# Attention pairs of four groups spread over both products of the groups before them, in a fused attention and feed-forward kernel

## The chip, the cores and the metric

The kernel runs on one core of a Trainium2 chip. The time is that of one execution on the device, in microseconds (us). Three runs of the kernel before gave 254.63, 254.75 and 253.64 us, a median of 254.63. A fourth execution was taken with the hardware profiler: 253.48 us, with 251.8 us from the first to the last instruction (the span). Of the engines, PE is TensorE (its weight loads are PEld), DVE is VectorE, ACT is ScalarE, POOL is GpSimd and SP is SyncE, which here only issues transfers.

## What is computed

Sliding-window attention with four sink keys, and behind it a two-layer network on all tokens:

```python
# q, k, v: (4 batches, 8 heads, 768 positions, 64), n_sink 4, window 128
scores = scale * np.matmul(q, k.transpose(0, 1, 3, 2))
keep = is_sink | in_window            # 0 <= row - column < 128, or column < 4
scores = np.where(keep, scores, -1e9)
a = np.exp(scores - np.max(scores, axis=-1, keepdims=True))
a = a / (np.sum(a, axis=-1, keepdims=True) + 1e-09)
attn = np.matmul(a, v)
x = attn.transpose(0, 2, 1, 3).reshape(3072, 512)
h = x @ w_in                          # 512 -> 2048
g = h * (1.0 / (1.0 + np.exp(-1.702 * h)))
out = g @ w_out                       # 2048 -> 512
```

## The kernel before

The 3072 tokens are cut into 12 groups g of 256 (two blocks i of 128); three groups t make one batch b. The eight heads are taken as four pairs hp. Everything stands in an order written out by hand: each engine runs its instructions in the order in which the program names them, so an instruction that waits holds all that stands behind it on that engine.

What one group needs, with the helper that issues it:

- `load_qk`, `load_v`: GpSimd issues the loads of 128 KB parts (line 124). `transposed_qk` (line 150 on) turns q and k: for g < EARLY = 3 by transposes on PE (L161) and copies by ACT (L163) and DVE (L165), for later groups by a DMA transpose on SP's queue (L154).
- `sinks(g)`: scores against the four sink keys on PE (L192), their scaled negatives and minima on DVE (L201 or L197, L203).
- `scores(g, hp)`: eight matmuls of a pair (L233, masks by L231) into PSUM. Groups in SPLIT (1 and 2) put the block before the diagonal into two `pr` tiles of the tag "av" and the block on the diagonal into a "nat" tile that two pairs share; other groups use one whole "nat" tile for a pair. There are two buffers of each tag: "nat", "av", and "mm" for the two products.
- `maxima(g, hp)` on DVE: the window chosen by a predicated copy (L247, or twice L256), the row maximum (L250, or L259) and the bias (L260).
- `weights(g, hp)` on ACT: four exponentials of 128x128 (L271). `sink_terms` (DVE, L302) and `sink_weights` (ACT, L311) do the same for the sink keys of all four pairs at once; `sink_transposed` turns them on PE (L316), with a copy on DVE (L318).
- `weights_transposed(g, hp, copy)`: on PE (L288) with a copy by DVE (L294) or ACT (L297), or without `copy` by a DMA transpose on SP's queue (L291).
- `upper` on POOL (L347) and `lower` on DVE (L329) or POOL cut the transposed weights into the two triangles. `values` (PE, L360, L368, L372) multiplies them with v; `normal` (DVE, L389, L390) divides.
- `x_transposed(g)` turns the attention output: on PE with one copy by ACT and one by DVE (L402, L404, L406) for g < EARLY, else by DMA (L408).

Then come the two products of a group. `hidden(g, F2)` for F2 = 0 to 7 is sixteen matmuls (L420) and one gelu on ACT (L423); `o(g, i, parts)` is four matmuls for each of four parts of the contraction (L435). `out_store` copies the result by ACT (L441) or DVE (L443) and stores it.

The first and second product alternate on PE, and the attention of the next group is put between them. In this text, round n runs from the first matmul of `hidden(n, 0)` to that of `hidden(n+1, 0)`; its first stage is the first product and its second stage the second product, each with what stands between. Rounds 0 and 1 are written out one by one; from round 2's first stage on the loop `for n in range(EARLY, NG + LAG2)` writes them (its pass n holds the second product of group n-2 and the first of group n-1). In rounds 0 and 1 the scores and maxima of the next group stand in the first stage, and its weights, values and division in the second; round 1's second stage also makes the scores and weights of group 3. In the loop the attention of group n is one round deeper: its weights are made beside the second product of group n-2, and its values beside the first product of group n-1; the scores of pairs 0 and 1 of the group after stand in the first stage, those of pairs 2 and 3 in the second.

ACT needs one table for exponentials and another for gelu, so it loads a table twice in a round. `sink_columns(b)` clears a tile of 128x1040 and sets its ones columns (L478, L479): for batch 0 at the start, for batch 1 in round 0's second stage, for batches 2 and 3 ahead of the loop.

Of the kernel before, what the change touches and what calls it, by code (L numbers as in the profile page):

```python
# [10 lines left out]
FP32 = mybir.dt.float32  # L11
FP16 = mybir.dt.float16
# [7 lines left out]
TG = 256  # L20
BIG = 1.0e9
LAG1, LAG2 = 1, 2
SPLIT = (1, 2)
EARLY = 3


# [32 lines left out]
def kernel(  # L59
# [48 lines left out]
        return psp.tile(list(shape), dt, tag="av", bufs=2, name=name)  # L108

    G = [dict() for _ in range(NG)]  # L110

    def load_part(g: int, part: int):

# [33 lines left out]
    def transposed_qk(g: int, parts=range(2)):  # L147
# [17 lines left out]
                        nc.vector.tensor_copy(out=T[:, bass.ts(a, HP)], in_=tp)  # L165
        G[g]["qkT"] = T.rearrange("p (e i c) s -> p e i c s", e=2, i=2)

    def sink_keys(b: int, copy):
        kT = G[b * NT]["qkT"]
        for h in range(2):  # L170
            copy(
                out=kd[b][bass.ts(h, D), :, bass.ts(h, n_sink)],
                in_=kT[bass.ts(h, D), 1, 0, :, 0:n_sink],
            )
# [31 lines left out]
    def scores(g: int, hp: int):  # L206

        b, t = divmod(g, NT)  # L210
        qkT = G[g]["qkT"]
        if g in SPLIT:
            if hp < 2:
                G[g]["both", hp] = psp.tile([P, 2, 2, 2, P], FP32, tag="nat", bufs=2, name=f"nat{g}_{hp}")
            two = G[g]["both", hp % 2]
            before = [av_bank(f"pr{g}_{hp}_{h}", (P, 2, P)) for h in range(2)]
            mine = [two[:, h, hp // 2] for h in range(2)]
            G[g]["mine", hp] = two[:, :, hp // 2]
        else:
            whole = psp.tile([P, 2, 2, 2 * P], FP32, tag="nat", bufs=2, name=f"nat{g}_{hp}")  # L220
            before = [whole[:, h, :, 0:P] for h in range(2)]
            mine = [whole[:, h, :, P:] for h in range(2)]
            G[g]["whole", hp] = whole
        for i in range(2):
            I = 2 * t + i
            prev = None if I == 0 else qkT[:, 1, 0, hp] if i else G[g - 1]["qkT"][:, 1, 1, hp]
            for to, keys in ((before, prev), (mine, qkT[:, 1, i, hp])):
                for h in range(2):
                    r = bass.ts(h, D)
                    if keys is None:  # L230
                        nc.tensor.matmul(to[h][:, i], masked_l[r], masked_r[r], start=True, stop=True)  # L231
                    else:
                        nc.tensor.matmul(to[h][:, i], qkT[r, 0, i, hp], keys[r], start=True, stop=True)  # L233
        G[g]["nat", hp], G[g]["before", hp] = mine, before
# [61 lines left out]
    def by_act(out_, in_):  # L296
        nc.scalar.copy(out_, in_)  # L297

    def sink_terms(g: int):
        sn, bias = G[g]["sn"], G[g]["bias"]  # L300
        ts_ = work.tile([P, 16, n_sink], FP32, tag="ts", name=f"ts{g}")
        nc.vector.tensor_tensor(  # L302
            out=ts_, in0=bias.rearrange("p i c h -> p (i c h)").unsqueeze(2).broadcast_to((P, 16, n_sink)),
            in1=sn, op=ALU.subtract,
        )
        G[g]["ts"] = ts_

    def sink_weights(g: int):
        ts_ = G[g]["ts"]
        As = sinkA[g % 2]  # L310
        nc.scalar.activation(out=As[:, 0:64], in_=ts_.rearrange("p a j -> p (a j)"), func=AF.Exp)  # L311
        G[g]["As"] = As

    def sink_transposed(g: int):
# [79 lines left out]
    def x_transposed(g: int):  # L394
        xT = work.tile([P, 2 * HP, P], FP16, tag="xT", bufs=3, name=f"xT{g}")
        xn = G[g]["xn"].rearrange("p i a h d -> p (i a h d)")
        if g < EARLY:
            bank = mm_bank if g == 0 else av_bank
            for i in range(2):
                tp = bank(f"tx{g}_{i}", (P, HP, P), FP16)  # L400
# [57 lines left out]
    masked_l = const.tile([P, P], FP16, name="maskedl")  # L458
    masked_r = const.tile([P, P], FP16, name="maskedr")
    sinkA = [const.tile([P, P], FP16, name=f"sinkA{i}") for i in range(2)]  # L460
    nc.vector.memset(vs[0], 0.0)
    nc.vector.tensor_copy(out=vs[0][:, :, D : D + 1], in_=sink_rows.unsqueeze(2))
    nc.vector.memset(masked_l, -1000.0)
    nc.vector.memset(masked_r, 15624.0)
    for t_ in (*kd, *sinkA):
# [1 line left out]
    for row in vn:  # L467
        for t_ in row:
            nc.vector.memset(t_[:, :, :, D : D + 1], 1.0)
    zero_reg = nc.gpsimd.to_reg(0.0)  # L470
    load_w_in(0)
    load_qk(1)
    load_v(0)
    for i in (1, 2, 3):
        load_w_in(i)

    def sink_columns(b: int):
        nc.vector.memset(vs[b], 0.0)  # L478
        nc.vector.tensor_copy(out=vs[b][:, :, D : D + 1], in_=sink_rows.unsqueeze(2))  # L479

    def ahead(n: int, hp: int):

# [50 lines left out]
    load_w_out(0)  # L533
    load_w_out(1)
    load_v(1)
    load_w_out(2)
    load_w_out(3)
    load_qk(2)
    load_v(2)


# [6 lines left out]
    sink_terms(1)  # L548


    sink_weights(1)
    sink_columns(1)
    weights(1, 0)
    weights(1, 1)
    o(0, 0, 0)
    sink_transposed(1)
    o(0, 1, 0)
    weights_transposed(1, 0, by_dve)
    upper(1, 0)
    weights(1, 2)  # L560
    o(0, 0, 1)
    weights_transposed(1, 1, by_dve)
    upper(1, 1)
    load_part(3, 0)
    lower(1, 0)
    weights(1, 3)
    o(0, 1, 1)
    weights_transposed(1, 2, by_dve)
    upper(1, 2)
    load_part(3, 1)  # L570
    values(1, 0)
    lower(1, 1)
    normal(1, 0)
    o(0, 0, 2)
    weights_transposed(1, 3, by_act)
    upper(1, 3)
    lower(1, 2)
    values(1, 1)
    normal(1, 1)
    o(0, 1, 2)  # L580
    lower(1, 3)
    values(1, 2)
    normal(1, 2)
    o(0, 0, 3)
    values(1, 3)
    normal(1, 3)
    out_store(0, 0)
    o(0, 1, 3)
    x_transposed(1)
    out_store(0, 1, act=True)  # L590
# [1 line left out]
    load_part(3, 3)  # L592
    load_v(3)
    transposed_qk(3)
    sink_keys(1, nc.gpsimd.tensor_copy)
    load_qk(4)


    for F2 in range(NF // 2):
        hidden(1, F2)  # L600
        if F2 == 0:
            transposed_qk(2)
        if F2 in (1, 2, 4, 6):
            ahead(2, (1, 2, 4, 6).index(F2))
    sink_terms(2)


    sink_weights(2)
    for hp in (0, 2, 1, 3):
        weights(2, hp)  # L610
        weights_transposed(2, hp)
        upper(2, hp)
        if hp in (0, 2):
            lower(2, hp, pool=True)
    sink_values(1)
    o(1, 0, 0)
    sink_transposed(2)
    o(1, 0, 1, 2)
    ahead(3, 0)
    o(1, 0, 3)  # L620
    out_store(1, 0)
    o(1, 1, 0)
    weights(3, 0)
    weights_transposed(3, 0)
    transposed_qk(4)
    scores(3, 1)
    lower(2, 1)
    maxima(3, 1)
    o(1, 1, 1)
    for hp in (0, 2):  # L630
        values(2, hp)
        normal(2, hp)
    o(1, 1, 2)
    scores(3, 2)
    lower(2, 3)
    weights(3, 1)
    weights_transposed(3, 1)
    for hp in (1, 3):
        values(2, hp)
        normal(2, hp)  # L640
    o(1, 1, 3)
    out_store(1, 1, act=True)
    x_transposed(2)
    maxima(3, 2)
    scores(3, 3)
    maxima(3, 3)
    sink_terms(3)
    weights(3, 2)
    weights_transposed(3, 2)
    weights(3, 3)  # L650
    weights_transposed(3, 3)
    sink_weights(3)
    load_qk(5)
    lower(3, 0)
    transposed_qk(5)
    sink_columns(2)
    sink_columns(3)

    for n in range(EARLY, NG + LAG2):
        att = n < NG  # L660
        g1, g2 = n - LAG1, n - LAG2

        if n > EARLY:
            if att and n + 1 < NG and (n + 1) % NT == 0:
                sink_keys((n + 1) // NT, nc.gpsimd.tensor_copy)
            if n in (4, 5):
                load_v(n)
            if att:
                for hp in (0, 1):
# [90 lines left out]
```

## Time and profile before

| | |
|---|---|
| median of three runs | 254.63 us (253.64 to 254.75) |
| profiled execution | 253.48 us, span 251.8 us |
| PE busy | 220.5 us (88%), 2180 matmuls |
| DVE, ACT, POOL busy | 151.5 us, 153.9 us, 101.6 us |
| granted TensorE clock, mean | 0.991 |

The rounds begin, by the first matmul of L420 in each, at 24.53 (round 0), 46.44, 73.25, 95.10, 113.85 and 130.98 us (round 5). Their second stages begin at about 34.33, 57.82, 87.32, 105.09 and 123.20 us. Rounds 5 to 10 take 16.8 to 17.3 us each, round 0 21.9, round 1 26.8, round 2 21.9 and round 3 18.8 us.

The profiler lists busy times; the waits are inferred from semaphore events. A matmul's end is modelled and lies behind the start of the next one, so the cost of a run of matmuls is read from start to start.

### The profile page before, as it was taken

How to read it: one execution, taken by the hardware profiler on the slowest of the kernel's cores; microseconds unless marked ns; L12 is line 12 of the kernel's file. 1: busy time of each engine (PE TensorE's matmuls, PEld its weight loads, DVE VectorE, ACT ScalarE, POOL GpSimd, SP SyncE). 2: the span in 40 equal slices, each digit the busy share in tenths (PEclk: the TensorE clock that was granted, in tenths of full speed). 3: DMA queues.
4: the chain of work that ended last, by engine and by line, in shares of the span. 5: the costliest groups of instructions: out<-in, count | busy, mean ns of one | idle time of the engine just before them, and what ended most of it. 6: DMA issues, size and time to landing. Idle time of an engine off the chain costs nothing.

```text
span 251.8 us, 5731 instructions
## 1 busy us (share of the span) xinstructions
PE 220.5 (88%) x2180; PEld 151.2 (60%) x2180; DVE 151.5 (60%) x397; ACT 153.9 (61%) x349; POOL 101.6 (40%) x154
## 2 busy tenths in 40 slices
PE   0437979797785999999999999999999999799993
PEld 0326756674354848738758569478486595494851
DVE  4686777386589647657768288477583783830101
ACT  2176575748457577676766875776777767751430
POOL 8848547423662825816624445356020220310000
PEclk9999999999998899999999999999999999999999
DMA  8999999989699999999999989999965623603102
GB/s 77 157 176 198 188 194 123 160 107 98 116 144 175 153 131 169 165 119 246 115 158 160 144 169 144 133 172 140 163 131 98 108 63 64 146 3 83 42 3 85
DMA packets 133612, 32.86 MB, mean 131 GB/s; under 512 B 126288, under 2 KB 130512, under 8 KB 133584
## 3 DMA queue, kind: packets, MB, share of 16 engines
q0 software_dynamic: 79104, 13.64, 73.7%
q1 hardware_dynamic: 54048, 18.73, 42.2%
q8 instruction: 17, 0.28, 0.5%
q10 hardware_dynamic: 432, 0.13, 0.2%
q14 instruction: 11, 0.09, 0.1%
HBM read 27.50 MB, written 6.29 MB: 134 GB/s over the span
## 4 chain that ended last, share of the span: by engine, by line
PE 51%; DVE 17%; ACT 16%; DMA 10%; issue 4%; POOL 0%; ACTq 0%; DVEq 0%; POOLq 0%; SPq 0%
PE hT L420 27%; PE o L435 12%; ACT A L271 7%; DVE m L250 5%; DVE nat L247 5%; DMA AT<-A 5%; ACT L423 4%; DMA xT<-xn 3%; PE av L372 2%; ACT L271 2%; ACT gT L423 2%; DMA qkn<-in_q_dram 2%; PE av L360 2%; PE av L368 2%; PE tqk L161 1%
## 5 line engine op out<-in xcount | busy, mean ns | idle before, releaser
L420 PE MATMUL hT<-xT,w_in 128*128 128x256 f16 x768 | 95.6, 275 | 5.4 <-ACT gT L423 2.4
L435 PE MATMUL o<-w_out,gT 128*128 128x512 f16 x384 | 89.6, 379 | 0.0
L420 PEld LDWEIGHTS <-w_in 128*128 128x128 f16 x768 | 72.8, 99 | 18.6 <-issue 3.5
L423 ACT ACTIVATE gT<-hT 128x512 f16<-128x512 f32 x96 | 56.5, 597 | 44.4 <-PE hT L420 44.2
L347 POOL TENSOR_SCALAR_AFFINE_SELECT up<-AT 128x512 f16<-128x512 f16 (+1 forms) x48 | 28.0, 588 | 103.6 <-DMA AT<-A 76.6
L271 ACT ACTIVATE A<-nat,bias 128x128 f16<-128x128 f32 x192 | 53.4, 383 | 24.4 <-DVE bias L260 19.2
L435 PEld LDWEIGHTS <-gT 128*128 128x128 f16 x384 | 34.9, 98 | 37.8
L247 DVE COPY_PREDICATED nat<-prev,nat 128x512 f32<-128x512 uint16 x40 | 27.7, 692 | 24.3 <-PE nat L233 11.1
L250 DVE TENSOR_REDUCE m<-nat 128x4 f32<-128x512 f32 x40 | 27.6, 691 | 1.4
L329 DVE TENSOR_TENSOR lo<-AT,own 128x512 f16<-128x512 f16 (+1 forms) x44 | 19.1, 448 | 5.8 <-DMA AT<-A 5.6
L124 POOL DMA_DIRECT2D qkn<-in_k_dram x24 | 21.3, 896 | 2.8 <-DMA w_out<-in_moe_w_out_dram 2.8
L124 POOL DMA_DIRECT2D qkn<-in_q_dram x24 | 21.6, 905 | 1.3 <-POOLq L741 0.8
L124 POOL DMA_DIRECT2D vn<-in_v_dram x24 | 21.2, 891 | 1.0 <-issue 0.8
L390 DVE TENSOR_TENSOR xn<-av,rcp 128x256 f16<-128x256 f32 x48 | 20.4, 424 | 1.7
L443 DVE COPY osb<-o 128x512 f32<-128x512 f32 x10 | 6.9, 691 | 23.2 <-PE o L435 23.2
L368 PE MATMUL av<-vn,up 128*128 128x65 f16 x160 | 18.6, 195 | 1.1 <-POOL up L347 1.1
L372 PE MATMUL av<-vn,lo 128*128 128x65 f16 x160 | 18.3, 196 | 0.7 <-POOL lo L347 0.6
L360 PE MATMUL av<-vs,AsT 128*128 128x130 f16 x80 | 16.6, 224 | 0.4 <-DVE xn L390 0.3
L389 DVE RECIPROCAL rcp<-av 128x4 f32<-128x4 f32 x48 | 8.5, 178 | 13.8 <-PE av L372 13.5
L368 PEld LDWEIGHTS <-up 128*128 128x128 f16 x160 | 14.9, 100 | 2.4 <-POOL up L347 1.3
L233 PE MATMUL nat<-qkT 64*128 64x128 f16 x272 | 16.0, 224 | 0.0
L233 PEld LDWEIGHTS <-qkT 64*128 64x128 f16 x352 | 11.4, 97 | 7.1 <-issue 6.9
(59 smaller groups left out, 184.6 us busy)
## 6 DMA issues: line engine op xcount, KB each, us to landing
out_dram<-osb SPq DMA_DIRECT2D x24, 256.0 KB
qkn<-in_q_dram POOLq DMA_DIRECT2D x24, 128.0 KB, 5.2
qkn<-in_k_dram POOLq DMA_DIRECT2D x24, 128.0 KB, 4.8
vn<-in_v_dram POOLq DMA_DIRECT2D x24, 128.0 KB, 6.4
w_in<-in_moe_w_in_dram POOLq DMA_DIRECT2D x4, 512.0 KB, 9.8
w_out<-in_moe_w_out_dram POOLq DMA_DIRECT2D x4, 512.0 KB, 10.1
AT<-A SPq DMA_TRANSPOSE x40
qkT<-qkn SPq DMA_TRANSPOSE x9
```

What stands on the lines that cost most here:

```text
L124: nc.gpsimd.dma_start(dst, (q, k, v)[e][b, :, rows].rearrange("h s d -> s h d"))
L233: nc.tensor.matmul(to[h][:, i], qkT[r, 0, i, hp], keys[r], start=True, stop=True)
L247: nc.vector.copy_predicated(out=nat[:, :, :, P:], mask=kinds(take_prev, g % NT), data=nat[:, :, :, 0:P])
L250: nc.vector.tensor_reduce(out=m1.rearrange("p h i -> p (h i)"), in_=nat.rearrange("p h i c -> p (h i) c")[:, :, P:], axis=AX.X, op=ALU.max,)
L271: nc.scalar.activation(out=A[:, 2 * h + i], in_=nat[h][:, i], func=AF.Exp, bias=bias[:, i, hp, h : h + 1], scale=scale,)
L347: nc.gpsimd.affine_select(out=out, in_=in_, pattern=[[0, rows], [sign, P]], compare_op=ALU.is_gt if sign < 0 else ALU.is_ge, fill=zero_reg ...
L360: nc.tensor.matmul(av[:, i].rearrange("p h d -> p (h d)"), AsT, vs[b][:, c : c + 2].rearrange("p h d -> p (h d)"), start=True, stop=False,)
L368: nc.tensor.matmul(av[:, i, h], up[:, h, i], vn[b][J // 2][:, J % 2, head], start=False, stop=False)
L372: nc.tensor.matmul(av[:, i, h], own_w[:, h, i], vn[b][t][:, i, head], start=(I == 0), stop=(I == 0 or h == 1))
L420: nc.tensor.matmul(hT[:, f], w_in16[:, c, bass.ts(F, P)], xT[:, :, c], start=(c == 0), stop=(c == 3))
L423: nc.scalar.activation(out=G[g]["gT"][:, 2 * F2 : 2 * F2 + 2].rearrange("p f s -> p (f s)"), in_=hT.rearrange("p f i s -> p (f i s)"), fun ...
L435: nc.tensor.matmul(o, gT[:, F, bass.ts(i, P)], w_out16[:, F], start=(F == 0), stop=(F == NF - 1))
```

## The change

The loop now starts with pass 5, which is round 4's first stage (LOOP = 5), and the attention of groups 2, 3 and 4 is written out, pair by pair, over both stages. In short:

- Round 0, second stage: group 1's weights are made in one go; three quarters of o's first two parts stand ahead of the sink transposes; group 2's q and k are transposed here in one tile of the tag "nat" (`transposed_qk_whole`); and group 2's sinks, scores, maxima and weights of pair 0 are made here, with the sink weights of that pair alone.
- Round 1, first stage: pair 0 of group 2 is finished up to its division, and pairs 1 to 3 get their scores and maxima. Second stage: weights, PE transposes, values and division of pairs 1 to 3 of group 2, and scores, maxima and weights (transposed by DMA) of pairs 0 and 1 of group 3.
- Round 2, first stage: scores and maxima of group 3's pairs 2 and 3, values of pairs 0 and 1, scores of group 4's pair 0. Second stage: pairs 2 and 3 of group 3 are finished, and pairs 0 to 2 of group 4 get maxima and weights.
- Round 3, in the same way: group 4's pair 3, then all of group 5. From round 4 on the loop is as before.
- `sink_terms` and `sink_weights` take a range of pairs and run twice for groups 2, 3 and 4 (on DVE two instructions each time); the transposes of the sink weights run twice as well.
- `x_transposed` uses PE for groups 0 to 4 (before: 0 to 2). Transposes of the weights of (2, all), (3, 2), (3, 3) and (4, 3) go by PE with copies, where before they went by DMA.
- All four `sink_columns` stand at the start, and the loads of group 2's q and k are issued ahead of the last two parts of w_out.

```diff
-SPLIT = (1, 2)
+SPLIT = {
+    (1, 0): (0, 0), (1, 2): (0, 1), (1, 1): (1, 0), (1, 3): (1, 1),
+    (2, 1): (2, 0), (2, 2): (2, 1), (2, 3): (3, 0),
+    (3, 2): (4, 0), (3, 3): (4, 1), (4, 0): (5, 0),
+}
+LOOP = 5
...
+    def transposed_qk_whole(g: int, copies):
+        n = G[g]["qkn"]
+        T = G[g]["qkT2"] = work.tile([P, 4 * HP, P], FP16, tag="qkT", bufs=4, name=f"qkT{g}")
+        tp = psp.tile([P, 4, HP, P], FP16, tag="nat", bufs=2, name=f"tqk{g}")
+        for a in range(4):
+            for c in range(HP):
+                nc.tensor.transpose(tp[:, a, c], n[:, a, bass.ts(c, P)], ident)
+        for a in range(4):
+            copies[a](T[:, bass.ts(a, HP)], tp[:, a])
...
-        if g < EARLY:
+        if g < 5:
             bank = mm_bank if g == 0 else av_bank
...
+    for b in range(B):
+        sink_columns(b)
...
     load_v(1)
+    load_qk(2)
     load_w_out(2)
     load_w_out(3)
-    load_qk(2)
...
     sink_weights(1)
-    sink_columns(1)
-    weights(1, 0)
-    weights(1, 1)
+    for hp in (0, 2, 1, 3):
+        weights(1, hp)
     o(0, 0, 0)
+    o(0, 1, 0)
+    o(0, 0, 1)
     sink_transposed(1)
...
+    transposed_qk_whole(2, (by_dve, by_act, by_dve, by_act))
...
+    sinks(2)
+    scores(2, 0)
     values(1, 2)
     normal(1, 2)
+    maxima(2, 0)
     o(0, 0, 3)
+    values(1, 1)
+    lower(1, 3)
+    normal(1, 1)
+    out_store(0, 0)
+    sink_terms(2, (0,))
+    weights(2, 0)
+    sink_weights(2, (0,))
     values(1, 3)
     normal(1, 3)
     o(0, 1, 3)
     x_transposed(1)
...
+    first_product(
+        1,
+        (sc(2, 1),),
+        (tr(2, 0, by_dve), lambda: upper(2, 0), sT(2)),
+        (sc(2, 2),),
+        (lo(2, 0),),
+        (av(2, 0),),
+        (sc(2, 3),),
+    )
+    sink_terms(2, (1, 2, 3))
...
+    sink_weights(2, (1, 2, 3))
+    for hp in (1, 2, 3):
         weights(2, hp)
...
+    ahead(3, 0)
     out_store(1, 0)
+    o(1, 1, 1)
+    weights_transposed(2, 3, by_act)
+    upper(2, 3)
+    scores(3, 1)
+    values(2, 1)
+    normal(2, 1)
     weights(3, 0)
     weights_transposed(3, 0)
+    values(2, 2)
+    lower(2, 3)
+    normal(2, 2)
+    o(1, 1, 2)
     maxima(3, 1)
+    sink_terms(3, (0, 1))
...
+    values(2, 3)
+    normal(2, 3)
     o(1, 1, 3)
+    x_transposed(2)
...
+    first_product(
+        2,
+        (sc(3, 2),),
+        (sT(3), lo(3, 0, 1)),
+        (sc(3, 3),),
+        (av(3, 0),),
+        (av(3, 1),),
+        (sc(4, 0),),
+    )
...
+    for hp in (2, 3):
+        weights(3, hp)
+    weights(4, 0)
+    o(2, 0, 0, 1, 2)
...
+    scores(4, 1)
+    maxima(4, 1)
+    out_store(2, 0)
+    o(2, 1, 1)
+    scores(4, 2)
+    values(3, 2)
+    normal(3, 2)
+    values(3, 3)
+    normal(3, 3)
+    weights(4, 1)
+    weights_transposed(4, 1)
+    maxima(4, 2)
+    sink_terms(4, (0, 1, 2))
+    o(2, 1, 2, 3)
+    weights(4, 2)
+    weights_transposed(4, 2)
+    sink_weights(4, (0, 1, 2))
+    x_transposed(3)
+    out_store(2, 1)
...
+    transposed_qk(5)
+    first_product(
+        3,
+        (sc(4, 3),),
+        (sT(4), lo(4, 0, 1)),
+        (av(4, 0),),
+        (lo(4, 2), sc(5, 0)),
+        (av(4, 1),),
+        (),
+        (av(4, 2),),
+    )
...
+    weights(4, 3)
+    weights(5, 0)
+    weights_transposed(5, 0)
+    transposed_qk(6)
+    o(3, 0, 0, 1, 2)
...
+    for n in range(LOOP, NG + LAG2):
```

In `first_product(g, ...)` the n-th tuple holds what is put behind `hidden(g, n)`: `sc` is scores with maxima, `tr` transposed weights, `sT` the sink transposes, `lo` the lower triangles, `av` values with the division.

## The prediction

> **What bounds the kernel now.** I read the busy time by stage first (columns: stretch, its length, busy time of PE, PEld, DVE, ACT and POOL with instructions, granted clock, DMA share, GB/s). Each stretch is a round, from one group's first hidden matmul to the next group's.
>
> ```profile
> 24.53:46.44 21.91, 19.84 (x210) 13.63 (x210) 15.63 (x40) 13.42 (x31) 13.94 (x18) 1.00 1.61 161
> 46.44:73.25 26.81, 22.17 (x242) 14.54 (x243) 16.82 (x43) 16.90 (x41) 12.08 (x18) 1.00 1.06 123
> 73.25:95.10 21.85, 18.50 (x166) 12.33 (x166) 15.11 (x39) 13.86 (x34) 8.61 (x13) 0.92 1.86 156
> 95.10:113.85 18.75, 17.53 (x179) 11.83 (x177) 12.64 (x30) 13.28 (x33) 10.22 (x16) 1.00 1.71 152
> 113.85:130.98 17.13, 17.13 (x178) 11.88 (x179) 12.07 (x29) 11.41 (x25) 9.16 (x15) 1.00 1.38 176
> ```
>
> From round 4 on PE is never idle. The lost time lies in rounds 0 to 3, 2.1, 4.6, 3.4 and 1.2 us of idle PE. What ends these waits (waits of PE: in total, times, longest):
>
> ```profile
> PE tAs L316 <- ACT sinkA L311: 4.3, 2, 2.4
> PE nat L231 <- ACT A L271: 2.9, 2, 2.5
> PE tAs L316 <- DVE vs L478: 1.4, 1, 1.4
> PE tAs L316 <- DVE vs L177: 1.4, 1, 1.4
> PE av L368 <- POOL up L347: 1.1, 1, 1.1
> ```
>
> The tAs waits are for the sink weights, which stand behind ACT's table load; the two put down to DVE also end where ACT's sink weights end (36.70 and 60.19 us). Round 2 also loses clock: in the stretches by single microseconds the granted clock is
>
> ```profile
> 80.00:81.00 1.00, 1.00 (x7) 0.74 (x6) 0.93 (x3) 0.12 (x1) 0.52 (x1) 0.51 0.67 10
> 81.00:82.00 1.00, 1.00 (x7) 0.69 (x6) 0.97 (x4) 0.48 (x1) 0.45 (x2) 0.50 1.02 214
> ```
>
> about half for some 3.4 us, after a stretch (75.2 to 79.5) in which PE did 0.9 us of work: some 1.7 us lost.
>
> **Unit prices**, from start to start: eight hidden or four output matmuls 0.87; scores of a pair 0.33; values 0.35; four transposes 0.22; from the end of PE's stream to its reader 0.2. On ACT: table 1.28, weights of a pair 1.06 to 1.14, sink weights 0.27, a copy 0.59. On DVE, from the timeline:
>
> ```profile
> 91.38 0.70 DVE L247 COPY_PREDICATED nat<-prev,nat 128x512 f32<-128x512 uint16 x1 [3.21 <-ACT A L271]
> 92.11 0.69 DVE L250 TENSOR_REDUCE m<-nat 128x4 f32<-128x512 f32 x1
> 92.83 0.17 DVE L260 SCALAR_TENSOR_TENSOR bias<-m,m 128x4 f32<-128x4 f32 x1
> 92.91 0.69 DVE L247 COPY_PREDICATED nat<-prev,nat 128x512 f32<-128x512 uint16 x1
> ```
>
> so a maximum is 1.54 (92.91 - 91.38); division 0.56, a lower triangle 0.34, transposed weights' copy 0.42, sink terms 0.25 in two parts (estimate from the 0.23 of one), xT copy 0.42.
>
> **The change stage by stage.** I follow the new order through each engine's queue.
>
> Start: three of the 0.93 + 0.17 us vs clears move ahead of DVE's first copy (5.81), which slips by about 1.1 us; the next PE-fed copy is at 9.24, with 1.6 us idle before it, so nothing later moves. Cost 0; without that cover 1.1. The loads of w_out's last half go behind four q and k loads: issue near 28 to 31, with 10.1 us to landing 38 to 41, use from 40.0. Cost 0, at most 1.5.
>
> Round 0, second stage (12.11 before). Removed: the 1.39 wait, since three output parts (2.6 us) now cover table and sink weights. Added on PE: 16 transposes 0.90, sinks 0.28, scores 0.33, and 0.7 waiting for the second pair's weights. What ends last is DVE's queue: `values(1,2)` starts at 43.3, DVE gets it at 43.9, then division 0.56, maximum (2,0) 1.54, lower (1,3) 0.34, division 0.56, sink terms 0.25, division 0.6 = 47.75; x transposes and copy 1.15: hidden(1) at 48.9, 2.5 later than before. Behind the lower triangle (1,3), which waits for the maximum, stand `values(1,3)` and the last output part on PE.
>
> Round 1, first stage (11.38): 8 x 0.87 + 3 x 0.33 + 0.28 + 0.35 = 8.6, plus 1.1 of waits on DVE (the copy of AT and lower (2,0) stand behind maxima) = 9.7: -1.7. The eight PE transposes of q that stood here are gone.
>
> Round 1, second stage (15.43). Gone: the DMA transposes of group 2's weights, whose landing held values. Now: gelu ends 59.4, table, sink weights and three pairs 64.15; on DVE copy to 64.05, sinks 0.5, maximum 1.54, division, lower, division 1.46, maximum 1.54, terms 0.25, division 0.6 = 69.95, transposes and copy 1.15: hidden(2) at 71.1, stage 12.5, -2.9.
>
> Round 2, first stage (14.07): 9.0 of PE work and 0.7 of waits, at full clock: 9.7, -4.4; it ends at 80.8. Second stage (7.78 before): gelu 81.6, table 82.9, sink weights 83.15, three pairs 86.35. DVE: copy and lower of (3,3) until 86.5, maximum (4,1) 1.54, two divisions 1.12, maximum (4,2) 1.54 = 90.7. Then ACT: weights (4,2) 1.14, sink weights 0.27, and only behind them the xT copy 0.59: hidden(3) at 92.85. 12.05 us, +4.3; PE stands idle for about 3 of them.
>
> Round 3, first stage (9.99): 9.0 + 0.5 = 9.5, -0.5. Second (8.76): table and weights to 106.85; DVE copy, lower, maxima (5,1), (5,2), (5,3) and a division end at 112.7, terms and copy: hidden(4) at 113.45, +2.3. ACT's next gelu ends at 116.65 behind weights (5,3) and the table, and the third block of hidden(4) needs it: 116.7, where before it started at 116.49. From there the order is the old one.
>
> Sum: +2.46 - 1.7 - 2.9 - 4.4 + 4.3 - 0.5 + 2.3 = -0.4 at hidden(4), +0.2 behind the gelu.
>
> Not in that walk: DMA landings. q and k of group 5 are turned by a DMA transpose issued near 93.4, behind the last store of group 2 on SP, and used at 98.0. The nearest row:
>
> ```profile
> 49.27 3.62 SPq L154 DMA_TRANSPOSE qkT<-qkn  x1
> 54.98 0.44 POOL L171 COPY kd<-qkT 64x16 f16<-64x16 f16 x2 [8.09 <-DMA qkT<-qkn]
> ```
>
> is 5.7 us from issue to reader: 99.1, +1.1 (0 to 3). Weights (3,1) are issued near 70.5 and read at 74.9, between maxima; such a landing took 2.5 us (61.29 to 63.8) to 6.5 us (90.39 to 96.9): 0 to 2, I take 0.5, nearer to the busy middle. Lower triangles beside POOL took up to 1.36 instead of 0.42; three on the chains: 0 to 1.5, I take 0, as the median row (0.417) says. The clock: 0, with one or two drops of 1.7 possible.
>
> [...]
>
> Total: +0.2 + 1.1 + 0.5 = +1.8, on 253.48 for the profiled execution; that one lies 1.15 below the median, and I compare medians: 254.63 + 1.8 = **256.4** us.
>
> **Rivals.**
> 1. Slower through the clock: round 2's idle second stage (from 89.9 to 92.85) starts a slow clock, one drop 256.4 + 1.7 = 258.1, two (round 1's end as well) 259.8. It decides if PE's work in such 3.4 us falls to the 0.9 seen at 75.2. For it: that row. Against it: the waits of 1.39 us cost no clock.
> 2. Faster: the ends of the second stages run at PE's pace, not DVE's. PE's work there is 12.6, 10.75, 9.9 and 9.65 us against my 14.6, 12.5, 12.05 and 11.1: 7.35 us less in all, 247.5. It decides where PE reaches the x transposes later than DVE's last division; about 60% of it gives 254.63 + 0.2 - 4.6 = 250.2. For it: DVE is busy only 15 of 22 us in a round, and in round 0 before no PE wait hung on a maximum. Against: the queues as written put 1.54 us maxima between a values and its division.
> 3. No change: all landings are in time and the walk holds, 254.63 + 0.2 = 254.8. For it: the 2.5 us landing; against: the 6.5 us one.
> That the spreading isn't there after building can be excluded: the built order of each engine has it.
>
> **How the numbers follow.** Forecast 0.34, rival 1 0.14, rival 2 0.33, rival 3 0.19. A change under 0.5% (1.3 us) can't be told from none here. Faster 0.33, same 0.19, slower 0.48. The forecast's own range is 255.9 to 259.5. The 8-in-10 range reaches into rival 2, to 249, leaving out its lower third, and up to 260.5, with two clock drops: the unknowns' upper bounds (1.9 + 1.5 + 1.5 + 1.5 above the sum) rarely fall together.
>
> **What would show it.** Right: round 0 near 24.4 us with PE waiting for a lower triangle or a division; round 1 near 22; round 2 near 22 with some 3 us before hidden(3) that end with ACT's xT copy; round 3 near 20.6 or more, sinks of group 5 waiting for qkT. Round 1's tAs waits and round 2's slow clock gone. Wrong: rounds 1 to 3 at 18 to 20 us with no PE wait over 1 us (rival 2), or a granted clock of half in round 2 or 3 (rival 1).

## The result and the profile after

The changed kernel took 261.32 us in the median of four runs (258.96 to 262.62), the kernel before 254.69 (253.64 to 255.93) beside it: a ratio of 1.026, with a 95% interval of 1.020 to 1.032. It is 6.6 us slower, outside the predicted range of 249 to 260.5. Its profiled execution took 260.94 us with a span of 259.0, which is 7.2 more than the span before. Ratios, here and below, leave out runs more than 1.5% above the fastest of their kernel, which the medians keep: the ratio of "maximum behind" stands on two of four runs (259.01 and 259.44 us), and its profile is of one left out. Lines have moved in the new file: the hidden matmuls are now L454, the output matmuls L469, the DMA transpose of q and k L160, that of x L442.

The busy time by rounds, after (the columns are those of the prediction's first fence):

```profile
24.32:48.54 24.22, 22.00 (x241) 15.27 (x242) 15.86 (x45) 15.73 (x38) 15.46 (x20) 1.00 1.52 156
48.54:70.74 22.20, 19.93 (x211) 13.70 (x212) 14.96 (x41) 15.05 (x37) 9.24 (x14) 1.00 1.06 104
70.74:93.48 22.74, 19.01 (x190) 12.68 (x191) 14.51 (x42) 14.51 (x36) 7.76 (x11) 1.00 0.93 91
93.48:115.48 22.00, 20.90 (x198) 13.45 (x197) 13.87 (x37) 13.17 (x30) 7.43 (x9) 0.92 1.08 120
115.48:133.97 18.49, 17.33 (x177) 11.85 (x178) 13.20 (x31) 13.49 (x34) 12.71 (x18) 1.00 1.87 151
133.97:154.72 20.75, 18.61 (x166) 12.33 (x167) 10.09 (x28) 11.45 (x25) 8.96 (x14) 0.92 1.89 164
```

Set against the rounds before, in us:

| round | 0 | 1 | 2 | 3 | 4 | 5 | 6 to 10 |
|---|---|---|---|---|---|---|---|
| before | 21.91 | 26.81 | 21.85 | 18.75 | 17.13 | 16.88 | 85.93 |
| predicted walk, without landings | 24.37 | 22.21 | 21.75 | 20.55 | 17.33 | 16.88 | 85.93 |
| after | 24.22 | 22.20 | 22.74 | 22.00 | 18.49 | 20.75 | 86.22 |

Rounds 0 and 1 together gain 2.3 us. Rounds 2 and 3 lose 4.1, rounds 4 and 5 lose 5.2. Two of the rounds have a mean clock of 0.92 where before there was one. Round 5, whose products and attention stand as before, is the largest single loss. (One thing in the loop did change, against "from round 4 on the loop is as before": v of groups 6 and 7 is now loaded at the start of passes 6 and 7, where before it was loaded three passes earlier.)

What ended PE's waits, after (totals over the whole execution, as before):

```profile
PE hT L454 <- ACT xT L438: 3.3, 2, 2.8
...
PE av L406 <- DMA vn<-in_v_dram: 2.1, 2, 1.4
...
PE av L406 <- DVE lo L363: 1.6, 2, 1.3
...
PE hT L454 <- DMA xT<-xn: 0.8, 1, 0.8
PE sk L210 <- DMA qkT<-qkn: 0.8, 1, 0.8
```

The first and third of these are the waits that the walk had placed, at the ends of rounds 2 and 0. Of the three for DMAs, a wait of 0.8 for xT was there before too, but ahead of hidden(4), at 113.85; now it stands ahead of hidden(5), at 133.97. Those for v and for qkT are new. In round 0 the timeline shows the chain that had been worked out, DVE first, then PE:

```profile
44.26 0.69 DVE L266 COPY_PREDICATED nat<-prev,nat 128x512 f32<-128x512 uint16 x1
...
45.79 0.42 DVE L363 TENSOR_TENSOR lo<-AT,own 128x512 f16<-128x512 f16 x1
...
46.27 0.20 PE L406 MATMUL av<-vn,lo 128*128 128x65 f16 x1 [1.29 <-DVE lo L363]
```

The maximum of group 2's pair 0 starts at 44.26, the lower triangle comes 1.53 us later, and PE waits 1.29 us for it. At the end of round 2, ACT and PE in the timeline:

```profile
91.68 1.14 ACT L290 ACTIVATE A<-nat,bias 128x128 f16<-128x128 f32 x4 [1.74 <-DVE bias L279]
...
92.83 0.60 ACT L438 COPY xT<-tx 128x512 f16<-128x512 f16 x1
...
93.48 1.86 PE L454 MATMUL hT<-xT,w_in 128*128 128x256 f16 x8 [2.79 <-ACT xT L438]
```

ACT's copy of xT starts at 92.83, only behind the weights of (4,2), and PE has waited 2.79 us for it. The eight matmuls that follow take 1.86 us instead of some 1.04. The granted clock is halved there; the stretch behind it:

```profile
94.00:95.00 1.00, 1.00 (x7) 0.60 (x5) 0.00 (x0) 0.73 (x1) 0.00 (x0) 0.50 1.93 131
```

Last, rounds 4 and 5. The chain of waits, after, between 110 and 143 us (start, duration, what):

```profile
110.18 6.39 DMA qkT<-qkn
...
116.62 0.20 POOL kd L189
...
127.20 1.67 POOL vn L130 x2
128.88 12.07 DMA vn<-in_v_dram
...
140.99 0.19 PE av L406
...
141.24 1.62 PE hT L454 x8
```

It runs from a DMA transpose of group 6's q and k over GpSimd to the load of v(6), which is issued at 127 to 129 and whose last part takes 12.07 us to land. PE waits for v(6) twice, 0.72 and 1.42 us, and behind that the clock is halved from 141.20 to 144.62, some 1.7 us lost (half of 3.41, an estimate). Together these are nearly the 3.87 us by which round 5 grew.

SP's queue says why the chain begins so late. After (a transpose of weights, those of q and k of groups 6 and 7, and that of x of group 5):

```profile
108.82 1.19 SPq L310 DMA_TRANSPOSE AT<-A  x1
110.18 3.32 SPq L160 DMA_TRANSPOSE qkT<-qkn  x1
...
122.97 3.50 SPq L160 DMA_TRANSPOSE qkT<-qkn  x1
126.57 1.27 SPq L442 DMA_TRANSPOSE xT<-xn  x1
```

and before:

```profile
98.55 1.32 SPq L154 DMA_TRANSPOSE qkT<-qkn  x1
...
115.67 3.15 SPq L154 DMA_TRANSPOSE qkT<-qkn  x1
...
124.07 1.23 SPq L408 DMA_TRANSPOSE xT<-xn  x1
```

The first of these transposes is issued 11.6 us later than before, the second 7.3 us later, and the x transpose behind it 2.5. What stands ahead of the first, the transpose of the weights of (5,0), had waited 10.9 us for ACT (waits of SP between 94 and 135 us):

```profile
SPq L310 <- ACT A L290: 11.1, 2, 10.9
```

On GpSimd the copies of the sink keys (L189) wait for that first transpose, and all loads behind them wait too:

```profile
116.62 0.44 POOL L189 COPY kd<-qkT 64x16 f16<-64x16 f16 x2 [5.41 <-DMA qkT<-qkn]
117.00 1.77 POOL L130 DMA_DIRECT2D qkn<-in_k_dram  x2
118.83 1.22 POOL L381 TENSOR_SCALAR_AFFINE_SELECT up<-AT 128x512 f16<-128x512 f16 x2
```

GpSimd stands still for 5.41 us, and then the loads of k(7) and the triangles of group 5 come at once.

### The profile page after: what moved, and what is told of

Same layout as the page of the kernel before. It is cut to its first block, busy times and chain, and to the rows that moved or that the text cites. A ratio compares the mean times of both kernels' runs of the same rounds, so it can differ in the third digit from the quotient of the medians.

```text
span 259.0 us, 5814 instructions
## 1 busy us (share of the span) xinstructions
PE 226.4 (87%) x2227; PEld 154.6 (60%) x2227; DVE 155.1 (60%) x417; ACT 156.0 (60%) x355; POOL 103.3 (40%) x152
## 3 DMA queue, kind: packets, MB, share of 16 engines
q1 hardware_dynamic: 48128, 17.29, 36.6%
## 4 chain that ended last, share of the span: by engine, by line
PE 49%; DVE 19%; ACT 13%; DMA 12%; issue 3%; POOL 3%; SPq 0%; ACTq 0%; DVEq 0%; POOLq 0%
PE hT L454 24%; PE o L469 14%; ACT A L290 7%; DMA qkT<-qkn 5%; DMA vn<-in_v_dram 5%; DVE m L269 5%; DVE nat L266 5%; ACT L457 2%; DMA AT<-A 2%; PE av L406 2%; DVE bias L279 1%; ACT gT L457 1%; DVE vs L496 1%; DVE xn L424 1%; PE av L394 1%
## 5 line engine op out<-in xcount | busy, mean ns | idle before, releaser
L454 PE MATMUL hT<-xT,w_in 128*128 128x256 f16 x768 | 97.2, 277 | 8.4 <-ACT xT L438 3.3
L469 PE MATMUL o<-w_out,gT 128*128 128x512 f16 x384 | 89.6, 379 | 0.0
L454 PEld LDWEIGHTS <-w_in 128*128 128x128 f16 x768 | 72.8, 99 | 22.2 <-issue 4.5
L290 ACT ACTIVATE A<-nat,bias 128x128 f16<-128x128 f32 x152 | 42.7, 374 | 24.7 <-DVE bias L279 21.4
L469 PEld LDWEIGHTS <-gT 128*128 128x128 f16 x384 | 35.0, 98 | 37.5
L266 DVE COPY_PREDICATED nat<-prev,nat 128x512 f32<-128x512 uint16 x38 | 26.3, 692 | 21.1 <-PE nat L252 11.4
L269 DVE TENSOR_REDUCE m<-nat 128x4 f32<-128x512 f32 x38 | 26.3, 691 | 1.3
L363 DVE TENSOR_TENSOR lo<-AT,own 128x512 f16<-128x512 f16 (+1 forms) x42 | 16.7, 411 | 5.9 <-DMA AT<-A 5.7
L406 PEld LDWEIGHTS <-lo 128*128 128x128 f16 x160 | 13.0, 99 | 2.1 <-DVE lo L363 2.1
```

Of the source, the lines that this page charges most:

```text
L266: nc.vector.copy_predicated(out=nat[:, :, :, P:], mask=kinds(take_prev, g % NT), data=nat[:, :, :, 0:P])
L269: nc.vector.tensor_reduce(out=m1.rearrange("p h i -> p (h i)"), in_=nat.rearrange("p h i c -> p (h i) c")[:, :, P:], axis=AX.X, op=ALU.max,)
L290: nc.scalar.activation(out=A[:, 2 * h + i], in_=nat[h][:, i], func=AF.Exp, bias=bias[:, i, hp, h : h + 1], scale=scale,)
L406: nc.tensor.matmul(av[:, i, h], own_w[:, h, i], vn[b][t][:, i, head], start=(I == 0), stop=(I == 0 or h == 1))
L454: nc.tensor.matmul(hT[:, f], w_in16[:, c, bass.ts(F, P)], xT[:, :, c], start=(c == 0), stop=(c == 3))
L469: nc.tensor.matmul(o, gT[:, F, bass.ts(i, P)], w_out16[:, F], start=(F == 0), stop=(F == NF - 1))
```

## The experiments

Eleven more kernels were run. The round lengths are those of each one's profiled execution, in us; the names are short for the headings below.

| kernel | 0 | 1 | 2 | 3 | 4 | 5 | 6 | median | ratio to before, interval |
|---|---|---|---|---|---|---|---|---|---|
| after | 24.22 | 22.20 | 22.74 | 22.00 | 18.49 | 20.75 | 17.29 | 261.32 | 1.026 (1.020 to 1.032) |
| late v | 21.90 | 26.73 | 21.84 | 18.17 | 17.20 | 17.16 | 18.83 | 253.80 | 0.995 (0.991 to 0.999) |
| v(6) early | 24.22 | 22.18 | 22.92 | 21.89 | 20.08 | 16.86 | 17.10 | 260.33 | 1.020 (1.010 to 1.030) |
| k(7) first | 24.22 | 22.18 | 22.97 | 22.70 | 20.13 | 16.63 | 17.28 | 259.68 | 1.018 (1.011 to 1.025) |
| weights behind x | 24.22 | 22.18 | 21.92 | 24.20 | 20.95 | 18.26 | 17.49 | 262.74 | 1.028 (1.020 to 1.035) |
| qk(6) early | 24.19 | 22.19 | 23.09 | 22.64 | 18.19 | 16.90 | 17.10 | 257.89 | 1.012 (1.005 to 1.018) |
| qk(6) and v(6) early | 24.19 | 22.19 | 22.56 | 22.49 | 17.48 | 17.38 | 17.37 | 258.20 | 1.014 (1.009 to 1.019) |
| maximum behind | 24.62 | 22.18 | 22.80 | 22.67 | 22.03 | 18.16 | 17.65 | 261.27 | 1.018 (1.011 to 1.024) |
| all moves | 24.62 | 22.17 | 21.57 | 20.73 | 17.62 | 16.82 | 18.36 | 255.40 | 1.002 (0.998 to 1.005) |
| moves, v(7) earlier | 24.21 | 22.18 | 21.89 | 20.73 | 17.64 | 17.03 | 17.45 | 254.68 | 1.002 (0.998 to 1.006) |
| pair 0 back | 22.45 | 24.21 | 21.91 | 20.73 | 17.53 | 16.82 | 17.96 | 254.70 | 1.003 (0.999 to 1.007) |
| cover only | 23.37 | 26.89 | 22.59 | 17.59 | 17.80 | 16.87 | 17.29 | 255.19 | 1.002 (0.998 to 1.006) |

Each kernel was timed beside the kernel before on its chip, and the chips differ a little (the kernel before has medians of 255.16, 254.73 and 253.67 us on three of them), so kernels are compared by their ratios.

### Late v alone, on the kernel before

```diff
-            if n in (4, 5):
+            if n in (4, 5, 6, 7):
                 load_v(n)
...
-                    if hp in (1, 2):
+                    if hp in (1, 2) and n > 4:
```

> The kernel before, with the values of groups 6 and 7 loaded at the start of passes 6 and 7, as in the changed kernel, instead of three passes ahead. Theory A (the late load of v alone makes round 5 slow: its landing holds values(6,0) on PE by some 2 us and the clock falls behind it): 1.5 to 4 us slower than the kernel before, 256 to 258.5 us, with a PE wait for vn in round 5. Theory B (round 5 is slow because everything is late after the new rounds 2 and 3, and the v load only shows it): within 1 us of before, no wait for vn over 0.5 us.

So v(6) and v(7) are loaded as late in the old kernel as in the new one. Measured: 253.80 against 255.16, and round 5 at 17.16, not 20.75 (round 6 rose to 18.83). PE has no wait for v in its profile. A late issue alone costs nothing that the timed runs show; by the ratio it is even slightly faster. So v's lateness is not by itself the cause of the new round 5. The landing differs too: the loads issued there take 4.2 to 6.4 us here, those of v(6) in after 9.5 to 12.1.

### v(6) early, in the new kernel

```diff
     load_part(7, 1)
+    load_v(6)
...
-            if n in (6, 7):
+            if n == 7:
```

> The changed kernel, with group 6's v loaded in round 3 behind the loads of group 7's q. Theory A: round 5 falls from 20.75 to about 17 us, 3 to 4 us faster than the changed kernel (257 to 258.5 us). Theory B (transfers are late as a whole): the wait moves to another transfer of the same round, at most 1 us gained.

Round 5 became 16.86, but round 4 rose from 18.49 to 20.08, and the interval of the ratio overlaps that of after. The wait had moved: in the waits of PE

```profile
PE hT L454 <- DMA xT<-xn: 2.4, 1, 2.4
```

and in the chain of waits of this kernel, the transpose of x that is issued at 128.17:

```profile
127.20 0.97 DVE vs L195
128.17 8.53 DMA xT<-xn
136.75 1.92 PE hT L454 x16
```

Without the late v, the next transfer that is late decides, and its landing takes 8.53 us. Rounds 4 and 5 together are 36.94 in the profile, 2.3 less than in after, in part because no half clock falls into them; the timed runs can't tell the two kernels apart.

### Loads of k(7) ahead of the sink keys' copies

```diff
     load_v(5)
-    sink_keys(2, nc.gpsimd.tensor_copy)
     load_part(7, 2)
     load_part(7, 3)
+    sink_keys(2, nc.gpsimd.tensor_copy)
     lower(5, 0)
```

> The changed kernel, with group 7's k loaded ahead of the sink keys of batch 2, which wait on GpSimd for a DMA transpose. Theory A (in round 4 the chain is sink keys, load of k, DMA transpose of group 7, and behind it on SP's queue the transpose of x of group 5): round 4 falls from 18.49 to about 17.3 us, the PE wait for xT (0.8 us) goes, 1 us faster than the changed kernel. Theory B (round 4 is late because ACT's weights of group 5 end late): round 4 stays within 0.4 us.

Round 4 stayed long, at 20.13, and round 5 fell to 16.63: again the same sort of shift (36.76 for both rounds, with no half clock), with the ratio's interval overlapping after's. The queue on GpSimd was freed of the loads, not of its wait; the sink scores still came late:

```profile
119.17 0.34 PE L210 MATMUL sk<-kd,qkT 128*128 128x8 f16 x8 [0.71 <-POOL kd L189]
```

The theory that the loads behind `kd` were the cost fell. The late transpose ahead of `kd` was left.

### The transpose of q and k of group 6 back to its earlier place

```diff
     sink_terms(4, (3,))
...
+    transposed_qk(6)
     sink_weights(4, (3,))
     weights(4, 3)
     weights(5, 0)
     weights_transposed(5, 0)
-    transposed_qk(6)
```

> The changed kernel, with the DMA transpose of group 6's q and k issued at the end of round 3's first stage, ahead of the weights of group 5's first pair, instead of behind their transpose (near 103 instead of 110.2 us). Theory C (the new order of SP's queue issues it 11.6 us later than before, the sink keys of batch 2 wait for it on GpSimd, and the loads and triangles behind them bunch in round 4): sink keys at once, triangles of group 5 near 115 us, round 4 at 17.1 to 17.6 us instead of 18.5 to 20, 1 to 2 us faster than the changed kernel. Theory D (the transpose of x lands late whenever loads are under way, wherever the others stand): the sink keys move, but PE still waits 1 to 3 us for xT, no gain over 0.7 us.

In the new kernel this transpose stands behind `weights_transposed(5, 0)` on SP, and so waits until ACT has made the weights of (4,3) and (5,0). One line moved up gives 257.89, a ratio of 1.012, whose interval (to 1.018) lies wholly under after's. The transpose is issued at 102.53, not 110.18. Round 5 is 16.90, and rounds 4 and 5 together are 35.09, where after has 39.24 and before 34.01. GpSimd's sink keys are no longer late, in the timeline of this kernel:

```profile
112.23 0.48 POOL L189 COPY kd<-qkT 64x16 f16<-64x16 f16 x2
```

4.4 us earlier than after and with no wait. The v(6) loads still are issued at 127 to 129, but land in 5.3 to 8.4 us, and PE doesn't wait for them. So the cause of most of the loss in rounds 4 and 5 is shown: one place on SP's queue, some 3.5 us of the 6.6. That includes the half clock of round 5, which had followed the wait for v(6). Round 3 stayed at 22.64.

### The same, and v(6) early

```diff
     load_part(7, 1)
+    load_v(6)
 
+    transposed_qk(6)
     sink_weights(4, (3,))
...
-            if n in (6, 7):
+            if n == 7:
```

> As the run before, and with group 6's v loaded in round 3 as well. Theory C: rounds 4 and 5 together fall from 39.2 us to about 34.5, near the 34.0 of the kernel before; 4 to 5 us faster than the changed kernel, 256 to 257.5 us. Theory D: the wait for xT stays, rounds 4 and 5 stay at 36.5 us or more.

The ratio of 1.014 is the same as without the v loads, within the intervals. Rounds 4 and 5 are 34.86 together (after 39.24, before 34.01, the previous kernel 35.09). The order of v adds nothing once the transpose is in time.

### Weights of (4,2) behind the x copy

```diff
     o(2, 1, 2, 3)
+    x_transposed(3)
     weights(4, 2)
     weights_transposed(4, 2)
     sink_weights(4, (0, 1, 2))
-    x_transposed(3)
```

> The changed kernel, with weights and sink weights of group 4's last pair behind the transpose of group 3's x in round 2, so that ACT copies x first. Theory A (ACT's order alone holds hidden(3) for 1.2 us, and this wait of 2.8 us brings the clock down at 93.6 us): hidden(3) starts near 92.2 instead of 93.48, the clock stays at 1.00 in round 3, 2 to 2.5 us faster than the changed kernel in runs where the clock had fallen. Theory B (DVE's maximum and the table load bind anyway): the wait moves behind gelu's table, under 0.7 us gained.

Round 2 fell by 0.8, and no half clock followed at once: at 93 to 99 us the granted clock is 1.00. But it is halved from 100.33 to 103.74 (the mean from 96 to 106 us is 0.83), round 3 rose from 22.00 to 24.20, and the whole did not gain. In the waits of PE:

```profile
PE hT L454 <- DMA xT<-xn: 3.3, 1, 3.3
...
PE sk L210 <- DMA qkT<-qkn: 2.7, 2, 1.7
```

Both are transposes on SP. The 1.7 is round 3's: the transpose of group 5's q and k is issued at 94.92, as in after (94.88), and PE, now earlier, waits for it until 99.36. The half clock follows that wait. The 3.3 stands at the end of round 4, ahead of hidden(5), again with a half clock behind it (a mean of 0.83 from 136 to 146 us). So x came earlier, and what it gained was given back to transfers that did not.

### The maximum behind the lower triangle

```diff
-    maxima(2, 0)
+    lower(1, 3)
     o(0, 0, 3)
     values(1, 1)
-    lower(1, 3)
     normal(1, 1)
+    maxima(2, 0)
```

> The changed kernel, with the maximum of group 2's pair 0 behind the lower triangle and division of group 1's last pairs in round 0. Theory A (DVE's order sets the end of the second stages: PE's wait of 1.29 us for the triangle hangs on this maximum): the wait for lo goes, hidden(1) starts 1 to 1.5 us earlier, at about 47.2 us. Theory E (PE's own work fills the stage, and the wait is only taken over by the next one): under 0.5 us earlier.

Round 0 did not shorten: 24.62, and the same in "all moves" below, which has this edit too. The 1.29 us wait for the lower triangle is gone, and in its place, ahead of the x transposes:

```profile
48.04 0.45 PE L436 MATMUL tx<-ident,xn 128*128 128x128 f16 x5 [1.71 <-DVE xn L424]
```

DVE has the same work to do before the last division, in whatever order. In these two orders the round's end is DVE's sum, not the place of one maximum.

### All moves together

```diff
     sink_terms(3, (2, 3))
+    transposed_qk(5)
     sink_weights(3, (2, 3))
...
-    transposed_qk(5)
     first_product(
         3,
```

To this come, as above, v(6) and qk(6) early, the weights of (4,2) behind the x copy, and the maximum behind. The move shown is new: the transpose of q and k of group 5 goes a stage earlier.

> All moves at once: q and k of groups 5 and 6 turned early, v of group 6 early, the maximum of round 0 behind, x of group 3 ahead of the last weights in round 2. Theories A and C: 1.3 + 2.3 + 4.5 us off the changed kernel, 252.5 to 254.5 us, no slower than the kernel before. Theory D: the moves give back what they gain in later transfers, 257 us or more.

The ratio is 1.002 (0.998 to 1.005): six of the 6.6 us are gone, and the kernel can't be told from the one before. Round 3 is 20.73, with the clock at 1.00 where it had been halved. The same microsecond, first in "qk(6) early", whose order of weights and x is after's, then here:

```profile
95.00:96.00 1.00, 1.00 (x12) 0.62 (x9) 0.49 (x1) 0.73 (x2) 0.00 (x0) 0.50 1.86 161
```

```profile
95.00:96.00 1.00, 0.79 (x8) 0.61 (x7) 0.93 (x4) 1.00 (x2) 0.00 (x0) 1.00 2.17 157
```

The x copy ahead of the weights did not pay alone; with the transposes in time the whole does, but what each of these moves is worth was not run apart. For round 3, which falls from 24.20 to 20.73, the transpose of group 5 is the likely one: its reader stands there, PE waited 1.66 us for it in "weights behind x", and here it does not wait.

### The moves without the maximum, and v(7) a pass earlier

```diff
-            if n == 7:
-                load_v(n)
+            if n == 6:
+                load_v(7)
```

> As the run of all moves, but with round 0 as the changed kernel has it, and group 7's v loaded a pass earlier (pass 6). Round 0 then takes 24.2 instead of 24.6 us and round 6 17.2 instead of 18.4, if the late v is what lengthened round 6: 253.5 to 254.5 us, 0.3 to 0.5% faster than the kernel before. If round 6's length came from elsewhere: 255 us.

The diff is against "all moves". The maximum is put back to the change's own place. Round 6 fell from 18.36 to 17.45, and round 0 from 24.62 to 24.21. The ratio is 1.002 again. The profile has one half clock, in round 2, in a place where after had none (below).

### Group 2's pair 0 out of round 0

```diff
-    (2, 1): (2, 0), (2, 2): (2, 1), (2, 3): (3, 0),
+    (2, 0): (2, 0), (2, 2): (2, 1), (2, 1): (3, 0), (2, 3): (3, 1),
...
-    sinks(2)
-    scores(2, 0)
...
-    maxima(2, 0)
...
-    sink_terms(2, (0,))
-    weights(2, 0)
-    sink_weights(2, (0,))
```

> As the run before it, with group 2's pair 0 taken out of round 0: its scores and maxima stand in round 1's first stage, its weights and values in round 1's second stage. Theory A (pair 0's work on DVE and ACT costs in round 0 what it saves in round 1): round 0 falls from 24.2 to about 22 us, round 1 grows from 22.2 to 23.5 to 24.5, the sum stays within 1 us. Theory F (spreading pays): round 1 grows by more than 3 us and the sum is over 1 us slower.

Sinks, scores, maximum and weights of that pair go to round 1. Against the kernel above, round 0 is 1.76 us shorter and round 1 2.03 longer: 46.66 for both, against 46.39. The ratios can't be told apart. Moving that pair into round 0 costs there nearly what it saves behind it.

### The cover of round 0 alone, on the kernel before

```diff
-    sink_columns(1)
-    weights(1, 0)
-    weights(1, 1)
+    for hp in range(HP):
+        weights(1, hp)
     o(0, 0, 0)
-    sink_transposed(1)
     o(0, 1, 0)
+    o(0, 0, 1)
+    sink_transposed(1)
+    o(0, 1, 1)
...
```

> The kernel before, with two parts of the change alone: three output parts ahead of round 0's sink transposes with the weights made in one go, and all four sink columns at the start. Theory A: the wait of 1.39 us in round 0 goes, round 0 takes 20.5 us instead of 21.9, the rest is as before: 253.3 us, 0.4 to 0.6% faster. Rival: the wait moves to the weights or the triangles, no gain over 0.4 us.

All sink columns go to the start, and more of the second product stands ahead of the sink transposes. The ratio is 1.002 (0.998 to 1.006), and round 0 is 23.37, 1.46 longer than before. The 1.39 us wait for the sink weights is gone from the second stage, but that stage takes 11.93 us instead of 12.11, since now the transposed weights and triangles are waited for (the longest such wait is 0.38 us). The loss is at the round's start, in PE's timeline:

```profile
24.66 1.87 PE L420 MATMUL hT<-xT,w_in 128*128 128x256 f16 x8 [0.61 <-DVE xT L406]
26.32 0.42 PE L161 MATMUL tqk<-ident,qkn 128*128 128x128 f16 x2
```

Eight matmuls take 1.66 from start to start, where before they took 0.87 (24.53 to 25.40). With the eight transposes and the eight matmuls behind them this is 3.84 us for work of 2.19. PE runs at half its rate up to some 28.1 us, though the column of the granted clock says 1.00 there. The traces explain it: their record of the clock begins at 22.00 us in the kernel before and at 21.73 in after, and the column shows a stretch without a record as 1.00. In these two the short matmuls of the values sped up (from 0.25 to 0.19 us each) between 21.7 and 22.0; here they are at 0.24 still at 22.25. The sink columns at the start are hardly the cause, as after has them there too; why the full rate came later in this execution is not shown. Some 1.65 us of round 0 here are that slow PE. Without them round 0 would be 21.7 (an estimate from these rows), and the cover is worth some 0.2, not the 1.39 that the prediction counted as removed.

## Why the prediction was right and wrong

**Start and rounds 0 and 1: right.** Round 0 begins at 24.32, not later than before, and PE waits for no load of w_out: both costs taken as 0 held. The walk gave 24.37 and 22.21, the profile 24.22 and 22.20. By stages of round 1 it gave 9.7 and 12.5, measured 9.72 (48.54 to 58.26) and 12.48 (58.26 to 70.74). PE waited for the lower triangle as said, and the tAs waits of round 1 are gone. Following DVE's queue instruction by instruction was the right method, against rival 2, for which the second stages should have run at PE's pace. "Maximum behind" shows for round 0 that it is DVE's sum.

**Round 2: the mechanism right, one landing missed.** The second stage took 12.16 (predicted 12.05), with PE's 2.79 us wait ending with ACT's copy of xT (predicted about 3). The first stage took 10.58, not 9.7: PE waited 0.78 for the transpose of group 4's q and k, a landing that the prediction did not look at. It priced the next one, qkT(5), which belongs to round 3.

**Round 3: a half clock on top of a landing that was priced.** The second stage took 11.13, predicted 11.1. The first took 10.87; the walk had 9.5, and 10.6 with the 1.1 for qkT(5). PE shows no wait for qkT(5), which was to be the sign, because the half clock brought PE to it late, at 99.54. In "moves, v(7) earlier", with a wait of 1.57 us ahead of hidden(3) and no half clock there, group 5's sink scores follow 4.78 us behind hidden(3) (92.89 to 97.67) and that stage takes 9.60; in after this would be 98.26. And in "weights behind x", with a whole clock up to there, PE waited for qkT(5) until 99.36, where the prediction had 99.1. So the two delays cover each other: of the 1.37 us above the walk some 1.1 were due by the landing alone (an estimate from these rows), and the clock adds little to it.

The clock's term of 0 was wrong all the same, and that it cost little in this place is luck. No run shows that term for a wait of about 3 us: in after the clock was halved from 93.42 to 96.83 us, behind the wait of 2.79. It was rival 1, held at 0.14, and its condition was met in the place that it named:

```profile
90.00:93.42 3.42, 0.69 (x10) 0.53 (x8) 2.71 (x7) 1.74 (x6) 1.54 (x3) 1.00 1.86 188
```

PE worked 0.69 us there, less than at 75.2 to 79.5 before (0.99 by the profile, in 4.3 us; the prediction says 0.9). The prediction has PE idle for about 3 us there and took this as harmless. The kernel before had a row against that, the longest single wait ahead of its drop (80.02 to 83.43 us), and the prediction should have gone by it:

```profile
77.56 0.23 PE L316 MATMUL tAs<-ident,sinkA 128*128 128x128 f16 x1 [2.41 <-ACT sinkA L311]
```

**"From there the order is the old one": this step failed, and it is the largest part.** With its landings of 1.6 the forecast has 90.48 us for rounds 0 to 3, measured 91.16. For rounds 4 and 5 it has 34.21, measured 39.24: they were taken as unchanged but for 0.2, and lost 5.2. But for the place of v(6) and v(7), the loop's instructions are the old ones. Yet the transpose of q and k of group 6, which used to be issued at 98.55, now stands in round 3's second stage behind transposed weights that wait 10.9 us for ACT, and goes at 110.18. What it holds up on SP and GpSimd ends in PE's waits for v(6) and a half clock. The prediction followed PE, DVE and ACT to hidden(4) and left SP's and GpSimd's queues at that point, though what those engines issue there is for the rounds behind. "qk(6) early" shows this cause: one line moved gives back some 3.5 us and brings rounds 4 and 5 to 35.09. "k(7) first" and "v(6) early" show that neither of the two things that the chain of waits names last is the cause, since each moved the wait to another transfer.

**The walk's net of -0.4: about right.** In "moves, v(7) earlier" rounds 0 to 3 take 89.01 us, before 89.32: 0.3 less, and each of the two profiles has one half clock among these rounds. That kernel also copies x of group 3 ahead of the last weights, which the walk did not have, so the agreement is in part luck. But the spreading, rid of late transfers, does about what the walk said: it takes 4.6 us out of round 1 and puts about as much into rounds 0 and 3. The rival of no change is what the change comes to with its queues in order: the moves take off about six of the 6.6.

**What stays open.** The price of one half clock is not known by itself. Round 3's first stage takes 10.76 to 11.57 in six profiles that have one at its start, and 9.60 in three without, but the landing of qkT(5) lies in the same difference. The runs' times say little: of the 13 runs of the kernel before beside "late v", the one with a mean clock of 1.000 took 253.93 us and the one with 0.978 took 254.58. Which part of round 4's 18.49 (17.6 in "all moves") is v(6)'s and which the transposes' was not separated. No version beats the kernel before by much: "late v" is at 0.995 with an interval that ends just under 1, and its edit is no part of the change.

## What to carry to other kernels

Work moved between stages moves its place on the queues of the engines that only issue transfers. For each moved DMA, name what now stands ahead of it there, and follow it as far as its reader's reader, past the point where the other engines' order is the old one. When a stage's end is the sum of one engine's work, spreading it over neighbours moves the time and does not remove it. A late transfer that the chain of waits names last may be only the next in line: put the earliest late one back first.

## What the runs showed of the hardware that was not expected

The same small transfers take very different times to land. v's loads of 128 KB in after, by the profile: 

```profile
DMA to landing us min/median/max: 3.8/7.0/12.1
```

and a transpose of x took 8.53 us in "v(6) early", issued at 128.17 while the loads of k and v, issued from 124.62 to 129.19, were under way.

The halving of the clock is not decided by the waits alone. At the end of round 1 after has waits of 1.29 and 0.55 us and "moves, v(7) earlier" 1.28 and 0.55, from the same instructions. In after the clock stays at 1.00; in the other it is

```profile
72.00:73.00 1.00, 1.00 (x11) 0.48 (x10) 0.00 (x1) 0.99 (x2) 0.42 (x2) 0.50 0.53 147
```

PE's work beside these waits does not tell the two apart either (the first of the busy times is PE's). The 3.41 us in "moves, v(7) earlier" that end with the drop, at 71.58, and in after those that end as far behind the first matmul of hidden(2):

```profile
68.17:71.58 3.41, 1.58 (x16) 1.08 (x15) 2.06 (x8) 2.35 (x8) 0.15 (x1) 1.00 1.41 115
```

```profile
67.91:71.32 3.41, 1.57 (x16) 1.08 (x15) 2.06 (x7) 2.35 (x8) 0.15 (x1) 1.00 1.42 115
```

Ahead of the other half clocks in the rounds of before and after PE worked as little or less: 1.51 us from 76.61 to 80.02 in before, and in after the 0.69 from 90.00 to 93.42 and 1.27 from 137.79 to 141.20. Each of these three half clocks lasted 3.41 us. What decided at the end of round 1 stays open. The runs of one kernel differ too: the 13 of before beside "late v" have mean clocks of 0.978 to 1.000. Every profile here but that of "all moves" has at least one half clock in its rounds (a mean clock of 0.997 there, of 0.983 to 0.993 in the others). At the start of a profile, ahead of the record's first entry, the granted clock is shown as 1.00 while PE may run at half its rate, as in "cover only" up to some 28.1 us (eight hidden matmuls in 1.66 us instead of 0.87): the spacing of known matmuls is the better sign there.
